# Attention into two dense layers on one core: bias load ahead of keys, another order of units in the last group, the weight split three steps earlier, and another end of attention

## The chip, the cores and the metric

The kernel runs on one core of a Trainium2 chip. The time is device microseconds (us) of one execution; lower is better. A run of the same kernel varies: the three runs of the kernel before lie between 447.11 and 455.0 us. Engines are called as the profile calls them: PE (TensorE matmul), PEld (its weight loads), DVE (VectorE), ACT (ScalarE), POOL (GpSimd) and SP (SyncE, which here issues DMAs; SPq is its queue).

## The reference

Three stages, in float32. Attention over 2 batches, 8 heads, 576 positions and head dimension 64, with a bias that a small network makes from positions; then a dense layer pair with softplus (512 to 2048 to 512); then a layer that sends each token to one of 8 experts or past them.

```python
scores = scale * np.matmul(q, k.transpose(0, 1, 3, 2))
x = (np.log1p(np.abs(rel)) / psi_i)[..., None]
bias = np.maximum(x @ w1 + b1, 0.0) @ w2
scores = scores + bias.transpose(2, 0, 1)[None, :, :, :]
attn = np.exp(scores - np.max(scores, axis=-1, keepdims=True))
attn = attn / (np.sum(attn, axis=-1, keepdims=True) + 1e-09)
attn_out = np.matmul(attn, v)
# ... tokens x 512, then
h = x @ w_in
y = (np.maximum(h, 0.0) + np.log1p(np.exp(-np.abs(h)))) @ w_out
# ... then the routed layer: gate, expert w1 and w2 of each token
```

## The kernel before

Rows of queries are cut into five tiles of 128 (the last, t = 4, has 64). Heads go in pairs (hp, four of them). A **unit** is one tile, one pair of heads and one batch; the half tile t = 4 takes both batches in one unit, called None. There are 36 units. Tiles form four groups, (0), (1), (2) and (3, 4), and the units of a group run pair by pair. For the pair hp = 0 of the last group the order is (3, batch 0), (3, batch 1), (4, both); for the other pairs the half tile comes first: (4, both), (3, batch 0), (3, batch 1).

The order of instructions on every engine is written out by hand up to the end of attention: a loop over steps n = 0 to 39 works on several units at once. In step n:

- DVE adds bias to the scores of unit n and finds their extreme (`maximum`, two instructions, j = 0 and 1); ACT takes the exponentials (`exp`); DVE makes reciprocals and POOL multiplies by them (`divide`). Up to step 16 the divide is in the same step, from LATE = 17 on in the next one.
- PE makes the scores of unit n + 1 (`sc`). The score tiles have two buffers, and one unit takes both.
- PE transposes unit n - 2 into `pt` (one buffer), and ACT copies it into the tile `at` (three buffers; one for each group, pair and batch).
- When all units that make up one (group, pair, batch) are done, three steps after the last of them PE multiplies by the values (`Values.product`, tile `po`, one buffer). In the next step ACT casts `po` to `x0hi` (`high`) and DVE subtracts into `x0lo` (`low`). Only then is `po` free. Of the first pair of the last group both batches are done with the same unit, so both products stand in step 29, the second after `high` and `low` of the first.
- Up to step 21 the bias of later tiles is made as well: DVE `hid`, PE `pb`, ACT `bsb`, and SP stores it in DRAM (`biasd`); SP loads it later for each tile and pair (`bias_load`), up to three units ahead.

Ahead of the loop the bias of tile 0 is made and stored in 8 pieces; then SP loads the second pair of keys (`k_load(1)`, two DMAs), the first values (`v_load(0)`), and the bias of pairs 0 and 1.

**The weight split.** The weights of the dense layers come as float64, and are turned into two float32 parts. `win_split` takes seven instructions for a block f of `w_in`: ACT `cin..m` (absolute value), DVE L130, L131, L132, L134 (`win`), ACT `whi`, DVE `wlo`. The blocks f = 0 to 3 are split during attention by `fill`: block f begins in step FILL + 4 f and ends four steps later; FILL is 23. Their raw loads (`raw_in`, two buffers) are issued by SP at steps FILL - 6 (two) and FILL + 4 f - 4. So block 3 ends in step 39. Blocks from 4 on are split by code behind attention, whose order a scheduler sets, and which may lie between the last instructions of attention.

Then comes the first dense layer: for each of 16 blocks f PE makes 36 matmuls into `ph` (L631, two buffers), ACT and DVE make the softplus (`ea`, `la`, `ua`, `gA`, `gBt`), and the block two further on can begin when `gA` and `gBt` (L648, L650) have read `ph`. Beside it the split goes on, of `w_in` blocks 4 to 15 and of `w_out` (`cout`, `wohi`, `wolo`). Tokens of groups 0 to 2 fill columns 0 to 767, those of the last group the rest; a block's last 12 matmuls read the rest.

Of the kernel before, what the change touches and what calls it, by code (L numbers as in the profile page):

```python
# [31 lines left out]
P = 128  # L32
# [12 lines left out]
LATE = 17  # L45
FILL = 23
DEPTH = 2
# [30 lines left out]
def build(ctx: ExitStack, tc: tile.TileContext, I, out, dbg=None):  # L78
# [84 lines left out]
    with ExitStack() as ac:  # L163
# [81 lines left out]

        def bias_load(t, hp):
            bt = ap3.tile([P, 2, S], F32, tag="bias", name=f"bias{t}_{hp}", bufs=4)
            src = biasd[t][:P * H * BW].rearrange("(q h w) -> q h w", h=H, w=BW)
            nc.sync.dma_start(bt, src[:, 2 * hp:2 * hp + 2, 16:16 + S])
            return bt  # L250
# [24 lines left out]
        class Unit:  # L275
# [33 lines left out]

            def divide(self):  # L310
                nc.vector.tensor_scalar(self.st[:, :, 2], self.st[:, :, 1], 1e-9, None, ALU.add)
                nc.vector.reciprocal(self.st[:, :, 3], self.st[:, :, 2])  # L312
                for j in range(2):
                    nc.gpsimd.tensor_scalar(self.ep[:, j], self.ep[:, j], self.st[:, j, 3:4], 0.0, ALU.mult, ALU.add)  # L314

# [39 lines left out]
        class Values:  # L355
# [4 lines left out]

            def product(self):
                n = group_cols(self.gi)[1]
                at, a5 = self.ats
                po = self.po = ps_o.tile([P, 512], F32, tag="po", name=f"po{self.gi}_{self.hp}_{self.b}")
                for c in range(4):
                    for j in range(2):
                        nc.tensor.matmul(po[64 * j:64 * j + 64, :n], vn[:, self.hp, c, self.b, j, :],  # L367
                                         at[:, j, c, :n], start=(c == 0), stop=False, tile_position=(0, 64 * j))
                for j in range(2):
                    nc.tensor.matmul(po[64 * j:64 * j + 64, :n], v5[:, self.b * 4 + self.hp, j], a5[:, :n],  # L370
                                     start=False, stop=True, tile_position=(0, 64 * j))
# [18 lines left out]
        for gi, ts in enumerate(GROUPS):  # L390
            for hp in range(4):
                for t in ts if hp == 0 else ts[::-1]:
                    for b in (range(B) if qrows(t) == P else (None,)):
                        units.append((gi, t, hp, b))
                        for b_ in range(B) if b is None else (b,):
                            ends[gi, hp, b_] = len(units) - 1
        qs, bts = {}, {}
# [23 lines left out]
        with tc.manual_schedule(engines=order | {nc.sync.engine}):  # L421
# [17 lines left out]
            for k in range(9):  # L439
                x = set_start(k, k % 2) if k < 8 else None  # L440
                if ready:
# [8 lines left out]
                    ready.store()  # L450
                ready = x
            k_load(1)
            v_load(0)
            bts[0, 0] = bias_load(0, 0)
            bts[0, 1] = bias_load(0, 1)
# [25 lines left out]
            for n in range(N + DEPTH + 2):  # L481
# [27 lines left out]

                for x in done[:1]:  # L510
                    x.high()
                if u:
                    u.maximum(0)
                    u.maximum(1)
                if lastV:
                    lastV.turned5()
                if lastU:
                    lastU.divide()
                for x in done[:1]:
                    x.low()  # L520
                fill(n, False)
                if cur:
# [8 lines left out]
                    cur.store()  # L531
                if u:
                    u.exp(0)
# [3 lines left out]
                if nxt:  # L537
                    nxt.room()
                    nxt.hidden(0)
                if u:  # L540
                    u.exp(1)
# [15 lines left out]
                for x in W[:1]:  # L557
                    x.product()
                if V:
# [4 lines left out]
                if u and n < LATE:  # L564
                    u.divide()
                if len(W) > 1:
                    W[0].high()
                    W[0].low()
                    W[1].product()
                    W = W[1:]  # L570
# [677 lines left out]
```

## Time and profile before

| what | value |
|---|---|
| time, median of 3 runs | 450.26 us (447.11, 450.26, 455.0) |
| the profiled execution | 446.41 us, its span 444.7 us |
| busy, share of the span | PE 94%, PEld 73%, DVE 75%, ACT 62%, POOL 16% |
| making of the first bias, start of the loop | to 29 us |
| attention, steps 0 to 39 | 29 to 179.5 us |
| first dense layer (L631) | 179.5 to 284 us |
| second dense layer | 284 to 350 us |
| routing and experts | 350 us to the end |
| granted TensorE clock | 0.997 of full speed (2.4 GHz), mean of the span |

Times in the trace count from the start of the span. Between the span and the profiled execution's time lie 1.7 us. The share of busy time is a mean over stages; what ends the wait of an engine in one stage stands in the brackets of the timeline's rows: idle time before the instruction, and who ended it.

### The profile page before, as it was taken

What the parts mean: (1) busy time and instruction counts of PE and PEld (TensorE: products, weight loads), DVE (VectorE), ACT (ScalarE), POOL (GpSimd) and SP (SyncE); (2) the same over time, 40 slices, a digit from 0 to 9 for tenths busy, and PEclk for the clock granted to TensorE, in tenths of its full rate; (3) what the DMA queues carried; (4) which work ended last, traced back from release to release, by engine and by line L of the source; (5) the groups of instructions that cost most, each with busy time, mean ns of one, the idle gap of its engine ahead of it and who ended that gap; (6) DMA issues with size and microseconds to landing.
All of it is one profiled execution on the core that took longest, in us unless ns stands there. A gap on an engine that the chain in (4) does not pass through costs nothing.

```text
span 444.7 us, 8978 instructions
## 1 busy us (share of the span) xinstructions
PE 419.5 (94%) x3355; PEld 324.7 (73%) x3355; DVE 332.5 (75%) x868; ACT 275.9 (62%) x519; POOL 70.9 (16%) x99
## 2 busy tenths in 40 slices
PE   8979999999999898979999999999999998999994
PEld 5325767676676566979999999977888776887741
DVE  5788788889878685799999999999995334625501
ACT  4787888888899687499988878936442332111010
POOL 3003332334346353000000000000000000201101
PEclk9999999999999999999999999999999999999998
DMA  6799964558875021642321301033340600599700
GB/s 169 206 334 361 312 190 141 165 138 277 232 248 193 27 95 47 200 139 76 109 83 60 96 0 49 1 99 105 129 142 1 247 38 1 217 360 405 279 1 22
DMA packets 38563, 66.60 MB, mean 150 GB/s; under 512 B 4272, under 2 KB 17844, under 8 KB 38512
## 3 DMA queue, kind: packets, MB, share of 16 engines
q1 hardware_dynamic: 37504, 64.38, 44.6%
q10 hardware_dynamic: 592, 0.80, 0.5%
q0 software_dynamic: 416, 0.77, 0.5%
q8 instruction: 28, 0.46, 0.4%
q14 instruction: 23, 0.19, 0.1%
HBM read 49.80 MB, written 16.69 MB: 150 GB/s over the span
## 4 chain that ended last, share of the span: by engine, by line
PE 54%; DVE 9%; ACT 4%; DMA 3%; issue 2%; POOL 0%; POOLq 0%; ACTq 0%; DVEq 0%; SPq 0%
PE ph L631 16%; PE px L664 5%; PE px L665 5%; PE px L666 5%; PE po L367 3%; PE sc L295 2%; PE bhA L971 2%; PE bhB L971 2%; PE byB L979 2%; PE pt L325 1%; DMA xbJ<-out_dram,tiJ 1%; PE sc_None L295 1%; DMA raw_in<-in_moe_w_in_dram 1%; PE prt L731 1%; DVE ua L652 1%
## 5 line engine op out<-in xcount | busy, mean ns | idle before, releaser
L314 POOL TENSOR_SCALAR ep<-ep,st 128x576 f32<-128x576 f32 x64 | 51.3, 813 | 101.3 <-DVE st L312 73.2
L631 PE MATMUL ph<-x0hi,whi 128*128 128x384 f32 x192 | 64.6, 337 | 2.8 <-DVE gBt L650 2.8
L631 PE MATMUL ph<-x0hi,wlo 128*128 128x384 f32 x192 | 64.2, 334 | 0.0
L631 PE MATMUL ph<-x0lo,whi 128*128 128x384 f32 x192 | 64.2, 334 | 0.0
L218 DVE TENSOR_SCALAR hid<-U 128x320 f32<-128x320 f32 (+17 forms) x134 | 55.3, 471 | 2.4 <-PE pb L223 2.3
L295 PE MATMUL sc<-kst,qr 64*128 64x288 f32 x256 | 51.5, 432 | 2.6 <-DVE st L301 1.2
L301 DVE CUSTOM_DVE_ANT_0 ep<-sc,bias 128x576 f32<-128x576 f32 x64 | 45.7, 751 | 5.1 <-POOL ep L314 2.0
L307 ACT ACTIVATE ep<-ep,st 128x576 f32<-128x576 f32 x64 | 49.0, 772 | 0.0
L295 PEld LDWEIGHTS sc<-kst,qr 64*128 64x128 f32 x256 | 28.8, 185 | 26.7 <-issue 12.7
L231 ACT ACTIVATE bsb<-pb,isc 128x287 f32<-128x287 f32 (+31 forms) x72 | 31.7, 493 | 19.3 <-PE pb L223 18.9
L367 PE MATMUL po<-at,vn 128*64 128x128 f32 (+1 forms) x512 | 38.4, 292 | 1.8 <-DVE x0lo L385 1.8
L223 PE MATMUL pb<-hid,pw 128*32 128x512 f32 (+18 forms) x320 | 38.4, 484 | 1.7 <-ACT bsb L231 1.6
L631 PEld LDWEIGHTS ph<-x0hi,whi 128*128 128x128 f32 x192 | 36.0, 188 | 4.3 <-ACT wohi L610 2.7
L631 PEld LDWEIGHTS ph<-x0lo,whi 128*128 128x128 f32 x192 | 36.0, 188 | 0.0
L631 PEld LDWEIGHTS ph<-x0hi,wlo 128*128 128x128 f32 x192 | 36.0, 188 | 0.0
L345 ACT COPY at<-pt 128x512 f32<-128x512 f32 x64 | 34.1, 587 | 1.4 <-PE pt L325 0.7
L367 PEld LDWEIGHTS po<-at,vn 128*64 128x64 f32 x512 | 28.9, 136 | 6.1 <-DVE x0lo L385 2.5
L325 PEld LDWEIGHTS pt<-ident,ep 64*128 64x128 f32 x512 | 26.5, 138 | 6.0 <-POOL ep L314 1.6
L325 PE MATMUL pt<-ident,ep 64*128 64x64 f32 x512 | 29.0, 226 | 1.2 <-ACT at L345 0.9
L672 ACT CAST ghiB<-gBt 128x384 fp32r<-128x384 f32 x16 | 8.2, 513 | 29.0 <-PE px L665 29.0
L664 PE MATMUL px<-wohi,ghiA 128*128 128x512 f32 x64 | 25.0, 391 | 0.0
L665 PE MATMUL px<-wolo,ghiA 128*128 128x512 f32 x64 | 25.0, 390 | 0.0
(415 smaller groups left out, 845.2 us busy)
## 6 DMA issues: line engine op xcount, KB each, us to landing
biasd<-bsb SPq DMA_DIRECT2D x40, 295.5 KB, 3.5
bias<-biasd SPq DMA_DIRECT2D x20, 576.0 KB, 6.1
raw_in<-in_moe_w_in_dram SPq DMA_DIRECT2D x16, 512.0 KB, 4.0
raw_out<-in_moe_w_out_dram SPq DMA_DIRECT2D x16, 512.0 KB, 3.3
ex<-in_moe_w_dram SPq DMA_DIRECT2D x8, 1024.0 KB, 12.3
ew<-in_moe_w_dram SPq DMA_DIRECT2D x4, 1024.0 KB, 6.0
qr<-in_p_q_dram SPq DMA_DIRECT2D x10, 256.0 KB, 4.7
kst<-in_p_k_dram SPq DMA_DIRECT2D x8, 288.0 KB, 5.4
```

Source lines behind the costliest of these rows:

```text
L218: nc.vector.tensor_scalar(self.hid[c][:, :self.R], U[:, :self.R], Lt[:, g:g + 1], 0.0, ALU.add, ALU.max)
L223: nc.tensor.matmul(ps[32 * c:32 * c + 32, :hi - lo], w2b, self.hid[c][:, lo:hi], start=True, stop=True, tile_position=(0, 32 * c))
L295: nc.tensor.matmul(self.sc[j][qs_, c, :288], self.q[js, self.hp, b, qs_], kst[js, self.hp, b, 288 * c:288 * c + 288], start=True, stop=Tru ...
L301: nc.vector.tensor_tensor_reduce(out=self.ep[:, j].rearrange("p (c k) -> p c k", c=2), in0=self.sc[j][:, :, :288], in1=bias.rearrange("p ( ...
L307: nc.scalar.activation(self.ep[:, j], self.ep[:, j], AF.Exp, bias=self.st[:, j, 0:1], scale=-1.0, accum_out=self.st[:, j, 1:2])
L314: nc.gpsimd.tensor_scalar(self.ep[:, j], self.ep[:, j], self.st[:, j, 3:4], 0.0, ALU.mult, ALU.add)
L325: nc.tensor.matmul(self.pt[:, r, c] if c < 8 else p5[r], flat[rs_, o:o + P], ident[rs_, rs_], is_transpose=True, start=True, stop=True, ti ...
L345: nc.scalar.copy(at.rearrange("p j c n -> p (j c) n")[:, :, off:off + 64], self.pt[:, r])
L367: nc.tensor.matmul(po[64 * j:64 * j + 64, :n], vn[:, self.hp, c, self.b, j, :], at[:, j, c, :n], start=(c == 0), stop=False, tile_position ...
L631: nc.tensor.matmul(ph[:, n, :384], ws[:, c, :], xs[xk][:, c, o:o + 384], start=(k == 0), stop=(k == 11))
L664: nc.tensor.matmul(px, ghi[:, cs], wohi[f], start=(f == 0), stop=False)
L665: nc.tensor.matmul(px, ghi[:, cs], wolo[f], start=False, stop=False)
```

## The change

Six edits. The first bias load is issued ahead of `k_load(1)` and `v_load(0)`, as two DMAs of one head each. FILL goes from 23 to 20. In the first pair of the last group the half tile goes between the two batches of tile 3. `high` is written behind `maximum`, and in the last unit's step (35) both exponentials come ahead of `high`. The last unit is divided on DVE, not POOL. The last product is put into the buffer `pb`, not `po`.

```diff
-FILL = 23
+FILL = 20
...
-        def bias_load(t, hp):
+        def bias_load(t, hp, parts=1):
...
-            nc.sync.dma_start(bt, src[:, 2 * hp:2 * hp + 2, 16:16 + S])
+            for j in range(0, 2, 2 // parts):
+                js = slice(j, j + 2 // parts)
+                nc.sync.dma_start(bt[:, js], src[:, 2 * hp:2 * hp + 2, 16:16 + S][:, js])
...
-            def divide(self):
+            def divide(self, eng):
...
-                    nc.gpsimd.tensor_scalar(self.ep[:, j], self.ep[:, j], self.st[:, j, 3:4], 0.0, ALU.mult, ALU.add)
+                    eng.tensor_scalar(self.ep[:, j], self.ep[:, j], self.st[:, j, 3:4], 0.0, ALU.mult, ALU.add)
...
-                for t in ts if hp == 0 else ts[::-1]:
-                    for b in (range(B) if qrows(t) == P else (None,)):
-                        units.append((gi, t, hp, b))
-                        for b_ in range(B) if b is None else (b,):
-                            ends[gi, hp, b_] = len(units) - 1
+                todo = [(gi, t, hp, b) for t in ts[::-1] for b in (range(B) if qrows(t) == P else (None,))]
+                if len(ts) > 1 and hp == 0:
+                    todo[:2] = todo[1::-1]
...
+            bts[0, 0] = bias_load(0, 0, 2)
             k_load(1)
             v_load(0)
-            bts[0, 0] = bias_load(0, 0)
             bts[0, 1] = bias_load(0, 1)
...
-                for x in done[:1]:
-                    x.high()
                 if u:
                     u.maximum(0)
                     u.maximum(1)
+                    if n == N - 1:
+                        u.exp(0)
+                        u.exp(1)
+                for x in done[:1]:
+                    x.high()
                 if lastV:
                     lastV.turned5()
                 if lastU:
-                    lastU.divide()
+                    lastU.divide(nc.vector if n == N else nc.gpsimd)
...
-                    x.product()
+                    x.product(*((ps_b, "pb") if n == N + DEPTH else (ps_o, "po")))
```

On SP, where the bias of tile 0 has been stored (`biasd_61` is tile 0's, `biasd_62` tile 1's; `bias_0` and `bias_1` are the pairs 0 and 1), it stands before as

```order
L244 DMA biasd_61<-bsb_288 16x8x591 x2
L259 DMA kst<-in_p_k_dram 64x2x576 x2
L262 DMA vn<-in_p_v_dram 128x1024
L249 DMA bias_0_308<-biasd_61 128x2x576
L249 DMA bias_1_310<-biasd_61 128x2x576
L244 DMA biasd_62<-bsb_336 16x8x591 x2
```

and with the change as

```order
L244 DMA biasd_61<-bsb_288 16x8x591 x2
L251 DMA bias_0_305<-biasd_61 128x576 x2
L261 DMA kst<-in_p_k_dram 64x2x576 x2
L264 DMA vn<-in_p_v_dram 128x1024
L251 DMA bias_1_311<-biasd_61 128x2x576
L244 DMA biasd_62<-bsb_337 16x8x591 x2
```

The load of pair 0, which waits until all stores of tile 0 have landed, now stands ahead of keys and values.

On PE, in steps 28 and 29 (names are tile, pair and batch, of `po` group, pair and batch; `sc4_2_None` are the scores of the half tile, 8 matmuls, of which the last stands here), before:

```order
L295 MATMUL sc4_2_None_1_2355<-kst_143,qr4_1958 64x288
L325 MATMUL pt4_1_None_2370<-ident_67,ep4_1_None_2201 128x64 x16
L330 MATMUL p5_29_2369<-ident_67,ep4_1_None_2201 128x128
L367 MATMUL po3_0_0_2389<-at3_0_0_2214,vn_144 64x192 x8
L370 MATMUL po3_0_0_2389<-a53_0_0_2215,v5_145 64x192 x2
L367 MATMUL po3_0_1_2403<-at3_0_1_2273,vn_144 64x192 x8
L370 MATMUL po3_0_1_2403<-a53_0_1_2274,v5_145 64x192 x2
L295 MATMUL sc3_2_0_0_2430<-kst_143,qr3_1805 128x288
```

and with the change, the end of step 28 first:

```order
L327 MATMUL pt3_0_1_2330<-ident_67,ep3_0_1_2159 128x64 x16
L332 MATMUL p5_28_2329<-ident_67,ep3_0_1_2159 128x128
L369 MATMUL po3_0_0_2349<-at3_0_0_2226,vn_144 64x192 x8
L372 MATMUL po3_0_0_2349<-a53_0_0_2227,v5_145 64x192 x2
L297 MATMUL sc4_2_None_0_2379<-kst_143,qr4_1891 64x288
...
L327 MATMUL pt4_1_None_2395<-ident_67,ep4_1_None_2213 128x64 x16
L332 MATMUL p5_29_2394<-ident_67,ep4_1_None_2213 128x128
L369 MATMUL po3_0_1_2414<-at3_0_1_2282,vn_144 64x192 x8
L372 MATMUL po3_0_1_2414<-a53_0_1_2283,v5_145 64x192 x2
```

The product of batch 0 moves one step up, to the other side of the scores `sc4_2_None`.

On ACT, at the end of attention (`ep3_3_1` is the last unit's), before:

```order
L381 CAST x0hi1_90<-po3_2_0_2658 128x192
L307 ACTIVATE ep3_3_1_2629,st3_3_1_2630<-ep3_3_1_2629,st3_3_1_2630 128x576 x2
L345 COPY at3_3_0_2683<-pt4_3_None_2688 128x8x64
L345 COPY at3_3_1_2685<-pt4_3_None_2688 128x8x64
L129 ACTIVATE cin3m_2721<-raw_in3_2459 128x512
L381 CAST x0hi1_90<-po3_2_1_2707 128x192
L345 COPY at3_3_0_2683<-pt3_3_0_2734 128x8x64 x2
L129 ACTIVATE cin4m_2879<-raw_in4_2875 128x512
L345 COPY at3_3_1_2685<-pt3_3_1_2757 128x8x64 x2
L381 CAST x0hi1_90<-po3_3_0_2776 128x192
L150 CAST whi3_101<-win3_2719 128x512
L381 CAST x0hi1_90<-po3_3_1_2792 128x192
```

and with the change:

```order
L309 ACTIVATE ep3_3_1_2639,st3_3_1_2640<-ep3_3_1_2639,st3_3_1_2640 128x576 x2
L383 CAST x0hi1_90<-po3_2_0_2668 128x192
L347 COPY at3_3_0_2692<-pt4_3_None_2697 128x8x64
L347 COPY at3_3_1_2694<-pt4_3_None_2697 128x8x64
L150 CAST whi3_101<-win3_2583 128x512
L383 CAST x0hi1_90<-po3_2_1_2716 128x192
L347 COPY at3_3_0_2692<-pt3_3_0_2739 128x8x64 x2
L129 ACTIVATE cin5m_2943<-raw_in5_2939 128x512
L347 COPY at3_3_1_2694<-pt3_3_1_2761 128x8x64 x2
L383 CAST x0hi1_90<-po3_3_0_2780 128x192
L129 ACTIVATE cin6m_3006<-raw_in6_3002 128x512
L383 CAST x0hi1_90<-po3_3_1_2795 128x192
```

The last exponentials stand ahead of the cast of `po3_2_0`, and blocks 5 and 6 of the weights stand where block 4 and nothing stood; `cin4m` is now eleven instructions further up, in step 33. On DVE 14 instructions stand between the last `x0lo` and the first `gA`, where there were 21; the seven that are gone from there stand ahead of it. On SP the raw load of block 6 moves ahead of the first two loads of `w_out`.

## Rows read from the trace of the kernel before

**Rows 1.** Busy time by stretch: us, engine busy (instructions), clock, DMA share, GB/s.

```profile
140.00:152.00 12.00, 10.07 (x121) 6.75 (x117) 8.30 (x28) 8.16 (x20) 5.05 (x6) 1.00 0.44 168
192.00:195.00 3.00, 0.62 (x4) 0.41 (x3) 3.00 (x6) 3.00 (x5) 0.00 (x0) 1.00 0.95 322
195.00:284.00 89.00, 88.58 (x508) 87.57 (x507) 87.52 (x134) 76.77 (x86) 0.00 (x0) 1.00 0.20 60
```

**Rows 2.** Timeline, step 0: start, duration, engine, line, operation; idle before and releaser.

```profile
28.81 0.80 PE L223 MATMUL pb<-hid,pw 128*32 128x352 f32 x8 [1.03 <-ACT bsb L231]
28.96 0.76 DVE L301 CUSTOM_DVE_ANT_0 ep<-sc,bias 128x576 f32<-128x576 f32 x1 [1.57 <-DMA bias<-biasd]
29.75 0.91 ACT L231 ACTIVATE bsb<-pb,isc 128x239 f32<-128x239 f32 x2 [1.00 <-PE pb L223]
```

**Rows 3.** Timeline: loads ahead of the loop on SP, and step 3's scores on PE.

```profile
19.99 1.31 SPq L259 DMA_DIRECT2D kst<-in_p_k_dram  x2
...
22.85 0.91 SPq L249 DMA_DIRECT2D bias<-biasd  x2
...
40.52 1.64 PE L295 MATMUL sc<-kst,qr 64*128 64x288 f32 x7 [0.29 <-PE pb L223]
```

**Rows 4.** Line 259 in the window 31.9 to 33.7 us: the two DMAs of k_load(2).

```profile
L259 SPq DMA_DIRECT2D kst<-in_p_k_dram x2: 639/782/925, 32.0 to 32.7; - x2
...
DMA to landing us min/median/max: 6.5/6.7/6.9
```

**Rows 5.** Timeline, steps 29 to 35: scores, the two products, and what they wait for.

```profile
144.85 1.87 PE L295 MATMUL sc_None<-kst,qr 64*64 64x288 f32 x16 [0.67 <-DVE st L301]
...
150.43 1.52 PE L367 MATMUL po<-at,vn 128*64 128x192 f32 x16 [1.03 <-DVE x0lo L385]
...
152.20 1.24 PE L295 MATMUL sc<-kst,qr 64*128 64x288 f32 x8
...
158.84 1.20 PE L295 MATMUL sc_None<-kst,qr 64*64 64x288 f32 x16
...
169.21 0.71 PE L325 MATMUL pt_None<-ident,ep_None 64*128 64x64 f32 x16
```

**Rows 6.** Timeline: DVE in steps 21 and 22, then the seven instructions of the first split.

```profile
118.68 0.27 DVE L385 TENSOR_TENSOR x0lo<-po,x0hi 128x128 fp32r<-128x128 f32 x1
120.99 0.76 DVE L301 CUSTOM_DVE_ANT_0 ep<-sc,bias 128x576 f32<-128x576 f32 x1 [2.04 <-POOL ep L314]
...
128.74 0.68 ACT L129 ACTIVATE cin0m<-raw_in 128x512 f32<-128x512 f32 x1
...
129.82 0.64 DVE L130 TENSOR_SCALAR cin0m<-cin0m 128x512 f32<-128x512 f32 x1
...
130.50 0.86 DVE L131 TENSOR_SCALAR cin0a<-cin0m 128x512 uint32<-128x512 uint32 x1
...
133.28 0.68 DVE L132 SCALAR_TENSOR_TENSOR cin0a<-raw_in,cin0a 128x512 uint32<-128x512 uint32 x1
...
136.65 0.84 DVE L134 SCALAR_TENSOR_TENSOR win<-raw_in,cin0a 128x512 uint32<-128x512 uint32 x1
...
138.92 0.63 ACT L150 CAST whi<-win 128x512 fp32r<-128x512 f32 x1
...
139.96 0.83 DVE L151 TENSOR_TENSOR wlo<-win,whi 128x512 fp32r<-128x512 f32 x1
```

**Rows 7.** Timeline, PE in steps 37 and 38: last transposes, last product.

```profile
174.14 0.71 PE L325 MATMUL pt<-ident,ep 64*128 64x64 f32 x16 [0.95 <-ACT at L345]
...
177.70 1.52 PE L367 MATMUL po<-at,vn 128*64 128x192 f32 x16 [0.81 <-DVE x0lo L385]
```

**Rows 8.** Timeline, start of the first dense layer.

```profile
178.31 0.37 SPq L142 DMA_DIRECT2D raw_in<-in_moe_w_in_dram  x1
...
182.67 0.66 ACT L129 ACTIVATE cin5m<-raw_in 128x512 f32<-128x512 f32 x1 [2.76 <-DMA raw_in<-in_moe_w_in_dram]
...
194.62 0.41 PE L631 MATMUL ph<-x0hi,whi 128*128 128x384 f32 x1 [2.38 <-DVE gBt L650]
```

More of the change, by code (lines that the diff above doesn't have):

```diff
@@ L359, in __init__, with product @@
                 self.gi, self.hp, self.b, self.ats = gi, hp, b, ats
-            def product(self):
+            def product(self, pool, tag):
                 n = group_cols(self.gi)[1]
                 at, a5 = self.ats
-                po = self.po = ps_o.tile([P, 512], F32, tag="po", name=f"po{self.gi}_{self.hp}_{self.b}")
+                po = self.po = pool.tile([P, 512], F32, tag=tag, name=f"po{self.gi}_{self.hp}_{self.b}")
                 for c in range(4):
@@ L391, in build @@
             for hp in range(4):
-                for t in ts if hp == 0 else ts[::-1]:
-                    for b in (range(B) if qrows(t) == P else (None,)):
-                        units.append((gi, t, hp, b))
-                        for b_ in range(B) if b is None else (b,):
-                            ends[gi, hp, b_] = len(units) - 1
+                todo = [(gi, t, hp, b) for t in ts[::-1] for b in (range(B) if qrows(t) == P else (None,))]
+                if len(ts) > 1 and hp == 0:
+                    todo[:2] = todo[1::-1]
+                for x in todo:
+                    units.append(x)
+                    for b_ in range(B) if x[3] is None else (x[3],):
+                        ends[gi, hp, b_] = len(units) - 1
         qs, bts = {}, {}
@@ L531, in build @@
                     cur.store()
-                if u:
+                if nu:
                     u.exp(0)
@@ L539, in build @@
                     nxt.hidden(0)
-                if u:
+                if nu:
                     u.exp(1)
@@ L564, in build @@
                 if u and n < LATE:
-                    u.divide()
+                    u.divide(nc.gpsimd)
                 if len(W) > 1:
@@ L568, in build @@
                     W[0].low()
-                    W[1].product()
+                    W[1].product(ps_o, "po")
                     W = W[1:]
```

## The prediction

> **What bounds the kernel now.** I read first the windows of busy time [rows 1]. In the first dense layer from 195 us on PE is busy 88.58 of 89 us at the full granted clock, so nothing placed there buys time, and an edit counts only where PE has holes. The same view shows two: 140 to 152 us, with PE busy 10.07 of 12, and 192 to 195 us, with 0.62 of 3 while DVE and ACT have no gap at all. The timeline of each hole, and of step 0, then says in its brackets who ended the wait. There the edits must act; each is priced by that wait and by what is late next. All sums are made against the profiled execution of 446.41 us; it lies 3.85 under the median of 450.26, so I add the difference to the median.
>
> **The first bias load.** In step 0 DVE's first extreme waits 1.57 us for the first bias load [rows 2]. That is what the edit attacks, but the wait is not on the path. Behind the extreme come the exponentials on ACT, and ahead of them ACT must copy the bias product: 29.75 for 0.91 us, after waiting 1.00 for PE's `pb` at 28.81, which itself waited for ACT [rows 2]. So the exponentials start at 30.6 however early the extreme is done at 28.96 + 0.76 + 0.75. I take a gain of 0; its far end is the whole 1.57.
>
> The price is on SP. The load leaves at 22.85, when the last store of tile 0 has landed; `k_load(1)` leaves at 19.99, ahead of that wait [rows 3]. Moved behind it, `k_load(1)`, `v_load(0)` and what SP issues after them start up to 22.85 - 19.99 = 2.86 us later. The first to feel it is `k_load(2)`: issued at 32.0 and 32.7, landing 6.5 to 6.9 later, so by 39.6 [rows 4]; the scores of step 3 start at 40.52 [rows 3]. The slack is 0.9. Some of the 2.86 may come back, because the moved transfers no longer run beside the last stores, which can then land earlier; I take a delay of 1.2, between 0 and 2.86 and nearer to the lower half, hence +0.3 past the slack (0 to 2.86 - 0.9 = 1.96). The edit as a whole: **+0.3**, bounds -1.57 and +1.96.
>
> The Trainium skill speaks against this edit: "DMA: Bandwidth & Descriptors", section "Anatomy of one DMA — SWDGE (gpsimd) path", states that DMA engines do not wait on semaphores and that any such wait happens on the issuing sequencer before dispatch. The issue at 22.85, with nothing from SP after `v_load(0)` until then, agrees [rows 3]. By that rule alone the edit would cost the whole 1.96; if loads could wait in the DMA engines it would cost 0.
>
> **The two products apart.** This is the main term. Three steps with one score of a half tile run from 144.85 to 158.84, 13.99 us, and hold the double product; the next three, which hold the same work but one product less, run from 158.84 to 169.21, 10.37 [rows 5]. The second product waits 1.03 for `x0lo` of the first, since `po` is one buffer, and takes until the next scores at 152.20, 1.77 after its start at 150.43 [rows 5]. With the half tile between the batches, batch 0 is multiplied in step 28 and batch 1 in 29: 3.62 leave the stretch, and 1.77 come back in step 28. There the scores wait 0.67 for DVE [rows 5], and the product now stands ahead of them and covers this wait if the extremes are not late themselves. So the saving is 3.62 - 1.77 = 1.85 to 1.85 + 0.67 = 2.52; the wait is one of DVE, which does not depend on the product, so I take **-2.4**. What is late next there: DVE's extremes, which already end the waits for scores.
>
> **The split three steps earlier.** The first block has seven instructions, 0.68 + 0.64 + 0.86 + 0.68 + 0.84 + 0.63 + 0.83 = 5.16 us [rows 6]; the other blocks meet the same kind of steps as before. The first now starts in step 20. DVE's share there, 0.64 + 0.86, comes behind `x0lo` at 118.68, ahead of the extreme at 120.99 that waits 2.04 for POOL [rows 6]: hidden, and without that wait 1.5. ACT's 0.68 stands ahead of a cast whose result `x0lo` needs, and may push it by a part. I take **+0.2**, bounds 0 and +1.0.
>
> **The end of attention** gains one wait and pays two small ones. The last product waits 0.81 at 177.70 for `x0lo` [rows 7]; in the buffer `pb` it needs not: -0.81. Against it, block 3's pair L130 and L131 now stands in step 33 ahead of the extremes; in rows it costs 0.64 + 0.86 = 1.5 beside POOL, and since `cin3m` may be early I take 0.9 (0 to 1.5). And `cin5m` now stands ahead of the last copies on ACT, while its raw load takes 4.36 from issue at 178.31 to the cast at 182.67 [rows 8]; issued as soon as block 3's `win` is done, it may hold up the copy and with it the last product. I take 0.6 (0 to 2.76, the wait it has now [rows 8]). The division on DVE is hidden behind the 0.95 that the last transposes wait for ACT's copy [rows 7]; were that cover gone, it would cost two instructions of the extreme's size, 0.76 each [rows 2], less POOL's. The exponentials ahead of `high` move `high` later, not the path: 0. Net **+0.7**, bounds -0.81 and +3.4.
>
> **The first dense layer.** PE waits 2.38 us at 194.62 for `gBt` of block 0 [rows 8], because ACT and DVE work off the late splits first: 3.00 of 3 us busy on both [rows 1]. With the split earlier, 14 instead of 21 DVE instructions stand between the last `x0lo` and the first `gA`; seven fewer at 0.43 to 0.86 are 3.0 to 6.0 us, more than the gap. But ACT at 182.67 waits 2.76 for a raw load [rows 8], and the next blocks' loads can bring such a wait back. I take **-2.2**, bounds 0 and -2.38.
>
> **Sum.** 0.3 - 2.4 + 0.2 + 0.7 - 2.2 = -3.4: a profiled execution of 443.0, and 450.26 - 3.4 = **446.9 us** at the median.
>
> **Rivals.** A, the start is on the path after all: if `pb` and the copies of step 0 do move up with the extreme, 1.57 is gained and 0.3 becomes about -1.6: sum -5.3, 445.0 us. Against it stands the order of ACT, where the copy precedes the exponential [rows 2]. Chance 0.12.
>
> B, the hole at 194.62 stays: the loads of block 6 and of the first of `w_out` land late, ACT stands in front of `ea`, and 2.38 is only passed on. The sum is -3.4 + 2.2 = -1.2, 449.1 us. For it speaks the 2.76 wait on a load [rows 8]. Chance 0.16.
>
> C, slower than before: the split moved into steps 20 to 24 is exposed. All 5.16 us on the path in place of 0.2 give -3.4 + 4.96 = +1.6, 451.9 us; it decides from 3.6 us exposed on. It would happen if ACT and DVE, not PE, set those steps. Against it stands the 2.04 in which DVE has nothing to do [rows 6]. Chance 0.10.
>
> D, the split of the products does nothing, as step 28 takes on as much as step 29 loses (its extremes late by the moved product): -3.4 + 2.4 = -1.0, 449.3 us. Against it stands the 1.03 wait, which has no reason to come back when the second product stands a step away. Chance 0.08.
>
> **How the numbers follow.** The forecast has 0.54. The range reaches from the forecast less the outer gains (-3.4 - 1.9 at the start = 445.0, and a further 3.5 for the scatter of the median: three runs lie between 447.11 and 455.0, the lowest 3.15 under the median) to C's 451.9: 441.5 to 452. The bound of 2%, about what a measurement of this kernel can tell from no change, is 441.3 and 459.3. All cases lie within it; faster by more needs A together with the best bounds of the tail (-0.8) and a low draw of the median: 0.11. Slower by more needs C with the bounds of start and tail: 0.03. Within: 0.86.
>
> **What would show it.** Right: the first extreme earlier by about 1.5 us while the first exponential stays at about 30.6; score starts of steps 29 to 32 about 10.4 us apart where they were 13.99, and no wait of PE for `x0lo` between two products; the first matmul into `ph` at about 178 (179.5 less 2.4, plus start, split and tail); no idle time ahead of block 2's first `ph`. Wrong: a wait of step 3's scores on a DMA of over 1 us; scores of steps 21 to 24 further apart; a wait of ACT for `raw_in` ahead of its last copies, or ahead of the first `ea`. The forecast fails on its largest terms, the products and the hole at 194.62, if either wait only moves to another engine.

## The result and the profile after

The changed kernel takes 443.3 us at the median of 20 runs (441.7 to 447.55), the kernel before 449.82 in the same comparison (446.39 to 455.5). The ratio is 0.9876, 95% interval 0.9855 to 0.9898: 1.2% faster, some 5.6 us; the medians lie 6.5 us apart, at the edge of that interval. The profiled execution takes 442.35 us with a span of 440.5; before it was 446.41 and 444.7. The 4.2 us between the spans can be followed by the start of each step's scores on PE, and this is where they arise:

| stretch | forecast, us | profiled, us |
|---|---|---|
| start, to the scores of step 4 | +0.3 | +1.31 (46.09 against 44.78) |
| the split in steps 20 to 24 | +0.2 | +0.04 |
| products, to the scores of step 31 | -2.4 | -2.53 (from +1.31 to -1.22) |
| end of attention, to the first `ph` | +0.7 | -0.39 (177.86 against 179.47, that is -1.61) |
| first dense layer, to block 2 | -2.2 | -2.12 (190.89 against 194.62, that is -3.73) |
| all behind it | 0 | -0.47 |
| sum | -3.4 | -4.2 |

The timeline of the changed kernel up to step 4, of SP, DVE, ACT and PE (start, duration, engine, line; in brackets idle time before and who ended it):

```profile
22.53 0.81 SPq L251 DMA_DIRECT2D bias<-biasd  x2
...
23.39 1.31 SPq L261 DMA_DIRECT2D kst<-in_p_k_dram  x2
...
27.34 0.74 DVE L303 CUSTOM_DVE_ANT_0 ep<-sc,bias 128x576 f32<-128x576 f32 x1
...
30.58 0.77 ACT L309 ACTIVATE ep<-ep,st 128x576 f32<-128x576 f32 x1
...
33.32 1.91 PE L297 MATMUL sc<-kst,qr 64*128 64x288 f32 x8 [1.80 <-DVE st L303]
...
34.72 1.53 SPq L261 DMA_DIRECT2D kst<-in_p_k_dram  x2
...
41.41 0.72 PE L297 MATMUL sc<-kst,qr 64*128 64x288 f32 x2 [0.35 <-DMA kst<-in_p_k_dram]
...
42.51 0.96 PE L297 MATMUL sc<-kst,qr 64*128 64x288 f32 x5 [0.38 <-DVE hid L218]
...
46.09 1.61 PE L297 MATMUL sc<-kst,qr 64*128 64x288 f32 x7
```

The same first exponential, `k_load(2)`, scores of step 1 and scores of step 4 in the kernel before:

```profile
30.55 0.77 ACT L307 ACTIVATE ep<-ep,st 128x576 f32<-128x576 f32 x1
...
31.97 1.62 SPq L259 DMA_DIRECT2D kst<-in_p_k_dram  x2
...
33.28 1.91 PE L295 MATMUL sc<-kst,qr 64*128 64x288 f32 x8 [0.85 <-DMA biasd<-bsb]
...
44.78 1.61 PE L295 MATMUL sc<-kst,qr 64*128 64x288 f32 x7
```

The first extreme comes at 27.34 instead of 28.96 and no longer waits for the bias load, but the first exponential starts at 30.58, where it started at 30.55. `k_load(2)` is issued at 34.72 instead of 31.97, 2.75 us later, and the scores of step 3, which did not wait for it [rows 3], now do: they start 0.89 later than the 40.52 of before, and stop for another 0.38 us at 42.51. The bracket there names a DVE instruction; that this was the second of the two DMAs of keys is read from its issue, 0.7 us behind the first, and not shown by a landing.

Two windows of busy time of the changed kernel (us, busy time of PE, PEld, DVE, ACT and POOL, granted clock, DMA share, GB/s):

```profile
20.00:22.50 2.50, 2.33 (x20) 0.62 (x18) 0.88 (x3) 0.75 (x2) 0.00 (x0) 1.00 0.69 209
...
35.36:38.70 3.34, 3.34 (x17) 1.85 (x13) 2.64 (x9) 1.99 (x5) 1.47 (x2) 0.50 1.05 410
```

The DMA engines have room while SP waits for the last store: their share is 0.69, where the same window of the kernel before has 0.94. From 35.36 to 38.70 the granted clock is 0.50, that is 1.2 GHz, behind the wait of 1.80 us at 33.32. In the kernel before, PE's wait ahead of the same scores was 0.85 us, and the clock stayed at 1.00.

The timeline from step 29 to the first dense layer, PE but for two rows of DVE and one of ACT:

```profile
147.26 1.20 PE L297 MATMUL sc_None<-kst,qr 64*64 64x288 f32 x16
...
151.06 1.24 PE L297 MATMUL sc<-kst,qr 64*128 64x288 f32 x8
...
157.62 1.20 PE L297 MATMUL sc_None<-kst,qr 64*64 64x288 f32 x16
...
162.17 0.73 DVE L130 TENSOR_SCALAR cin3m<-cin3m 128x512 f32<-128x512 f32 x1
162.94 0.43 DVE L131 TENSOR_SCALAR cin3a<-cin3m 128x512 uint32<-128x512 uint32 x1
...
164.09 1.67 PE L297 MATMUL sc<-kst,qr 64*128 64x288 f32 x7 [0.67 <-DVE st L303]
...
169.77 1.52 PE L369 MATMUL po<-at,vn 128*64 128x192 f32 x16 [0.35 <-DVE x0lo L387]
...
173.43 0.71 PE L327 MATMUL pt<-ident,ep 64*128 64x64 f32 x16 [0.91 <-ACT at L347]
...
174.15 0.68 ACT L129 ACTIVATE cin5m<-raw_in 128x512 f32<-128x512 f32 x1 [0.77 <-DMA raw_in<-in_moe_w_in_dram]
...
176.09 1.52 PE L369 MATMUL po<-at,vn 128*64 128x192 f32 x16
...
177.86 0.44 PE L638 MATMUL ph<-x0hi,whi 128*128 128x384 f32 x1
...
190.89 0.41 PE L638 MATMUL ph<-x0hi,whi 128*128 128x384 f32 x1 [0.25 <-DVE gBt L657]
```

From 147.26 to 157.62 are 10.36 us where 13.99 stood [rows 5]: the three steps have become as long as the next three. The last product has no wait (it was 0.81 [rows 7]), and ahead of block 2 stand 0.25 instead of 2.38 us [rows 8]. The first `ph` of the kernel before started at 179.47:

```profile
179.47 0.44 PE L631 MATMUL ph<-x0hi,whi 128*128 128x384 f32 x1
```

### The profile page after: what moved, and what is told of

The parts are those of the page before. It is cut to its first block, busy times and chain, and to the rows that moved or that the text cites. A ratio compares the mean times of both kernels' runs of the same rounds, so it can differ in the third digit from the quotient of the medians.

```text
span 440.5 us, 8980 instructions
## 1 busy us (share of the span) xinstructions
PE 418.5 (95%) x3355; PEld 324.7 (74%) x3355; DVE 333.5 (76%) x870; ACT 275.9 (63%) x519; POOL 70.2 (16%) x97
## 4 chain that ended last, share of the span: by engine, by line
PE 52%; DVE 12%; ACT 4%; DMA 3%; issue 2%; SPq 0%; POOL 0%; POOLq 0%; DVEq 0%; ACTq 0%
PE ph L638 14%; PE px L671 5%; PE px L672 5%; PE px L673 5%; PE po L369 3%; PE sc L297 2%; DMA raw_out<-in_moe_w_out_dram 2%; PE bhA L978 2%; PE bhB L978 2%; PE byB L986 2%; DMA xbJ<-out_dram,tiJ 1%; DVE hid L218 1%; PE sc_None L297 1%; DVE ua L659 1%; PE pt L327 1%
```

## The experiments

Twelve kernels ran. A stretch is read from the profile, since executions differ in slow stretches of the clock (last section) by more than most single edits are worth. Each ratio is to the kernel before, with its 95% interval.

**The first bias load back behind the first values**, the rest as changed:

```diff
-            bts[0, 0] = bias_load(0, 0, 2)
             k_load(1)
             v_load(0)
+            bts[0, 0] = bias_load(0, 0)
```

> The changed kernel with the first bias load put back behind the first values, as before. Theory (the moved load costs 1.30 us between steps 0 and 4): first extreme at about 28.96 again, no granted clock of 0.50 between 35 and 39 us, scores of step 4 at 44.8 instead of 46.09, all later steps 1.3 us earlier; profiled execution about 441.0, ratio to the kernel before about 0.985. Rival (the delay of steps 2 to 4 is due to something else, or is taken back later): scores of step 4 stay at about 46, or the end stays at 442.3, ratio 0.9876.

The timeline and a window of this kernel:

```profile
40.64 1.64 PE L297 MATMUL sc<-kst,qr 64*128 64x288 f32 x7 [0.29 <-PE pb L223]
...
44.90 1.62 PE L297 MATMUL sc<-kst,qr 64*128 64x288 f32 x7
...
373.50:377.00 3.50, 3.50 (x10) 2.68 (x10) 3.33 (x19) 0.51 (x1) 0.00 (x0) 0.51 0.20 18
```

Scores of step 4 at 44.90, no wait for keys, and the last matmul `ph<-x0hi,whi` starts at 278.5 instead of 280.1: the theory holds in all that it can be read from. The profiled execution still takes 442.45, because the clock falls in the routing, at 373.5, and that costs 1.6. Median 442.01, ratio 0.9859 (0.981 to 0.9908): 0.8 us better than 0.9876, with an interval of some 2 us either way, so the two can't be told apart.

**The moved load alone**, in the kernel before (the diff above read the other way round):

> The kernel before with the first bias load moved ahead of keys and values, as in the change, and nothing else. Theory (the moved load pushes k_load(2) past the slack of 0.9 us, and the wait makes the clock fall in some executions): first extreme at 27.3, first exponential still at 30.6; scores of step 4 between 46.0 and 48.5 instead of 44.78, varying from execution to execution; slower than the kernel before by 1.3 to 3.5 us, ratio 1.003 to 1.008. Rival (the start costs only inside the changed kernel, or is taken back in the first steps): scores of step 4 at 44.8, ratio 1.000 or below.

PE's scores in its timeline:

```profile
33.19 1.91 PE L297 MATMUL sc<-kst,qr 64*128 64x288 f32 x8 [1.80 <-DVE st L303]
...
43.30 2.62 PE L297 MATMUL sc<-kst,qr 64*128 64x288 f32 x7 [2.83 <-DMA kst<-in_p_k_dram]
...
48.99 1.41 PE L297 MATMUL sc<-kst,qr 64*128 64x288 f32 x6
```

Slower: 453.46 against 449.77, ratio 1.007 (1.0035 to 1.0105), some 3.1 us. The wait of 2.83 is the one for `k_load(2)`, and the matmuls behind it run at a granted clock of 0.56 to 0.59 from 43 to 47 us. Scores of step 4 come at 48.99, 4.2 us late and half a microsecond later than the theory's end. Five of the profiled kernels have this same code up to step 4 (this one, the changed kernel, and three below); their step 4 stands at 46.09, 46.68, 47.77, 48.99 and 50.11, on average 3.1 us behind 44.78. So the 1.31 of the changed kernel's profile is the cheapest of five draws.

**Exponentials of step 0 ahead of the bias copy on ACT**, in the changed kernel:

```diff
                     u.maximum(1)
-                    if n == N - 1:
+                    if n in (0, N - 1):
                         u.exp(0)
                         u.exp(1)
...
-                if nu:
+                if nu and n:
                     u.exp(0)
...
-                if nu:
+                if nu and n:
                     u.exp(1)
```

> The changed kernel with both exponentials of step 0 ahead of the copy of the bias product on ACT. Theory (the early extreme is worth nothing since ACT takes the copy first, and k_load(2) is the next limit): first exponential at about 28.8 instead of 30.58, scores of step 1 at about 31.8 instead of 33.32 and no slow clock behind them; but the scores of step 3 wait for k_load(2), which lands at 41.3 and about 42.4, so the scores of step 4 come at 45.6 to 46.1 instead of 46.09 and the whole at 441.8 to 442.4, ratio 0.986 to 0.988. Rival (the price of the load was the clock alone): scores of step 4 at 44.5 or earlier, the whole at about 440.8, ratio 0.984.

ACT and PE in the timeline of this kernel:

```profile
28.63 0.77 ACT L309 ACTIVATE ep<-ep,st 128x576 f32<-128x576 f32 x1
...
31.80 1.73 PE L297 MATMUL sc<-kst,qr 64*128 64x288 f32 x8
...
41.54 2.53 PE L297 MATMUL sc<-kst,qr 64*128 64x288 f32 x7 [2.07 <-DVE hid L218]
...
48.46 1.24 PE L297 MATMUL sc<-kst,qr 64*128 64x288 f32 x8
```

The first two parts of the theory show: exponential at 28.63, scores of step 1 at 31.80, 1.5 us earlier. So it was ACT's order that withheld the gain of the early extreme. Step 3 then waits 2.07; the bracket names a DVE instruction that had ended, and `k_load(2)` landed at 41.40, just ahead of the start at 41.54. Step 4 at 48.46 is later than either theory gave: behind the longer wait the clock stays at 0.50 for 6 us. Median 443.71, ratio 0.9882 (0.9825 to 0.9939).

**The same with `k_load(2)` right behind the first two bias loads**, ahead of the values:

```diff
             k_load(1)
+            bts[0, 1] = bias_load(0, 1)
+            k_load(2)
             v_load(0)
-            bts[0, 1] = bias_load(0, 1)
...
-                if n < 2:
-                    k_load(n + 2)
+                if n == 1:
+                    k_load(3)
```

> The changed kernel with both exponentials of step 0 ahead of the copy of the bias product, and the keys of the third pair, k_load(2), issued right behind the first two bias loads instead of in step 0. Theory (the early extreme is worth 1.5 us only if nothing behind it waits for the loads that were pushed back): scores of step 1 at 31.8, of step 3 at about 39.2 without a wait, of step 4 at 43.3 to 43.6 where the changed kernel has 46.09 and the kernel before 44.78; granted clock 1.00 from 30 to 46 us; profiled execution about 439.7, or 441.3 if a slow stretch of the clock falls into the routing. Rival (the load of the values, now behind, is the next limit, or DMA is full until 54 us anyway): scores of step 4 at 45 or later, no better than the kernel before.

PE and DVE in the timeline of this kernel:

```profile
39.83 1.64 PE L297 MATMUL sc<-kst,qr 64*128 64x288 f32 x7 [0.29 <-PE pb L223]
...
44.09 1.61 PE L297 MATMUL sc<-kst,qr 64*128 64x288 f32 x7
...
52.90 0.76 DVE L303 CUSTOM_DVE_ANT_0 ep<-sc,bias 128x576 f32<-128x576 f32 x1 [1.13 <-DMA bias<-biasd]
```

No wait for keys at step 3, and step 4 at 44.09, half a microsecond behind the theory but 0.69 ahead of the kernel before. Then, at 52.90, an extreme waits 1.13 for a later bias load, and from step 6 on the kernel is 0.6 behind the kernel before. The rival's sign, step 4 at 45 or later, did not come; its reason fits what came instead: from 30 to 54 us the DMA engines of the kernel before have a share of 1.06, so that what is moved ahead may make another transfer late. No run shows this apart. The profiled execution, 443.26 with a slow stretch in the routing, is 2 us above the 441.3 expected. Ratio 0.9853 (0.9795 to 0.9912).

**Ten idle matmuls in PE's wait of 1.80 us** (added work that nobody reads):

```diff
+                    if n == 1:
+                        idle = ps_o.tile([P, 512], F32, tag="po", name="idle")
+                        for k in range(10):
+                            nc.tensor.matmul(idle[:, :P], ident, ident, start=True, stop=True)
                     nu.scores()
```

> The changed kernel with ten matmuls of 128 by 128 in step 1 whose result nobody reads, in the 1.80 us in which PE waits ahead of the scores at 33.32. Theory (half of the 1.30 us is the clock that fell behind that wait, half the late k_load(2)): clock 1.00 from 35 to 39 us, scores of step 2 at 36.4 to 36.5, of step 3 at about 41.3, where k_load(2) lands, of step 4 at about 45.5 to 45.7 instead of 46.09. Rival 1 (the clock cost nothing that k_load(2) would not cost anyway): scores of step 4 at 46.0. Rival 2 (all of it is the clock): scores of step 4 at 44.8.

PE at step 3 in the timeline of this kernel:

```profile
45.27 2.67 PE L297 MATMUL sc<-kst,qr 64*128 64x288 f32 x7 [4.93 <-DMA kst<-in_p_k_dram]
```

Inconclusive. The added matmuls take 2.50 us and put the scores of step 1 at 33.95 instead of 33.32. The clock stays at 1.00 from 33 to 43 us, but in this execution `k_load(2)` was issued at 37.01 and landed at 45.1, and the wait of 4.93 swallowed what was to be told apart; step 4 stands at 52.19. Ratio 0.9897 (0.9832 to 0.9962). In the changed kernel's own profile the split of its 1.31 can be read without it: `k_load(2)` landed at 41.28, step 3 began at 41.41, so with a full clock it could have begun 0.13 earlier. There the late keys are the price, and the slow clock ran beneath it.

**The new order of units alone**, in the kernel before:

> The kernel before with the new order of units alone. Theory (one product moved saves 2.5 us and needs none of the other edits): scores of step 30 at 149.7 instead of 152.20, the rest of attention 2.5 us earlier, first dense layer from 177.0; the hole ahead of block 2 stays at 2.4 us or grows a little; profiled execution about 443.9, ratio 0.9945. Rival (the gain needs the split out of these steps): scores of step 30 at 151 or later, ratio 0.997 or more.

PE in the timeline of this kernel, at step 30 and at block 2:

```profile
149.94 1.24 PE L295 MATMUL sc<-kst,qr 64*128 64x288 f32 x8
...
193.22 0.41 PE L633 MATMUL ph<-x0hi,whi 128*128 128x384 f32 x1 [2.48 <-DVE gBt L652]
```

Scores of step 30 at 149.94 where 152.20 stood, while step 24 is 0.20 later: 2.47 us saved, as expected, and by one edit. In the next step 0.31 is lost to an extreme that is late beside the split, so that 2.16 are left, and another 0.45 goes in step 34 in the same way (a wait of 0.65 at 163.33). So the first dense layer starts at 177.96, a microsecond later than expected. The hole of 2.48 remains. Profiled 446.48 with a slow stretch of 1.6 in the routing, where 443.9 was expected; ratio 0.996 (0.9921 to 0.9999).

**FILL = 20 alone**, in the kernel before:

> The kernel before with the split begun three steps earlier and nothing else. Theory (the split's place decides the hole ahead of block 2 of the first dense layer, 2.38 us): hole of 0.3 us or less, steps 20 to 24 not later by more than 0.2 us, profiled execution about 444.3, ratio 0.995. Rival 1 (the last unit's edits closed the hole): hole above 1.5 us, ratio 0.999. Rival 2 (the split is exposed in the last steps of attention): hole closed, but the first dense layer starts at 180.2 or later, ratio 0.997 or more.

PE in the timeline of this kernel, at step 34 and at the first dense layer:

```profile
164.62 1.67 PE L295 MATMUL sc<-kst,qr 64*128 64x288 f32 x7 [0.67 <-DVE st L301]
...
179.39 0.45 PE L631 MATMUL ph<-x0hi,whi 128*128 128x384 f32 x1
```

No row of the first dense layer in this timeline has a wait in brackets: the hole is gone, by this edit alone. Steps 20 to 24 are not later (0.10 us behind the kernel before, and 0.05 before them), steps 29 to 33 are 0.7 earlier, because the wait of 0.67 ahead of the scores at 144.85 [rows 5] is gone; it is the one that the moved product covers, so the two edits do not add up there. Of the 0.7, 0.47 goes at 164.62, where the extremes stand behind the pair L130 and L131. Ratio 0.9911 (0.9871 to 0.9951), the largest of the parts.

**FILL = 23 in the changed kernel**:

> The changed kernel with the split begun in step 23 again. Theory (the split's place alone closes the hole ahead of block 2, and costs two tenths in steps 20 to 24): attention no later, first dense layer from 177.4 to 177.9, but a wait of 2.2 to 2.8 us ahead of block 2 in place of 0.25; total about 2.2 us longer, ratio 0.992. Rival (the order of the last steps closes it as well): wait below 1.2 us, ratio 0.989 or less.

PE at step 34, at a product of step 35 and at block 2 in the timeline of this kernel:

```profile
164.81 1.67 PE L297 MATMUL sc<-kst,qr 64*128 64x288 f32 x7 [0.65 <-DVE st L303]
...
171.01 1.52 PE L369 MATMUL po<-at,vn 128*64 128x192 f32 x16 [0.86 <-DVE x0lo L387]
...
193.98 0.41 PE L638 MATMUL ph<-x0hi,whi 128*128 128x384 f32 x1 [2.25 <-DVE gBt L657]
```

The hole is back with 2.25 us; ratio 0.9951 (0.9908 to 0.9994), 3.4 us slower than the changed kernel's, where 0.992 was expected. The first dense layer starts at 178.97, outside the expected 177.4 to 177.9 and 1.11 behind the changed kernel: 0.59 of it comes from the start (step 4 stands at 46.68), and 0.51 from the product at 171.01, which waits 0.86 for `x0lo` where the changed kernel waits 0.35. The wait of 0.65 at step 34 is there as well, with the split in its old place. Behind the hole the granted clock falls to 0.50, from 195 to 197 us.

**The last product in `po` again**:

```diff
-                    x.product(*((ps_b, "pb") if n == N + DEPTH else (ps_o, "po")))
+                    x.product(ps_o, "po")
```

> The changed kernel with the last product in the buffer po again. Theory (the other buffer saves the wait of 0.81 us): a wait of 0.8 us for x0lo ahead of the last product, first dense layer from 178.6 to 178.7 instead of 177.86, the rest of attention unchanged, total 0.8 us longer if the hole ahead of block 2 does not take it up (it has 0.25 left). Rival (ACT's copy behind block 5 is late anyway): start of the dense layer unchanged within 0.2 us.

The last product in the timeline of this kernel:

```profile
178.89 1.52 PE L369 MATMUL po<-at,vn 128*64 128x192 f32 x16 [0.81 <-DVE x0lo L387]
```

The 0.81 is back to the digit. From the scores of step 34 to the first `ph` it takes 165.99 to 180.67, 14.68 us, against 13.77 in the changed kernel (and 14.63 before). The start at 180.67 instead of 178.6 is mostly due to a late step 4 (47.77 instead of 46.09). Ratio 0.9925 (0.9888 to 0.9962).

**The last unit divided on POOL**:

```diff
-                    lastU.divide(nc.vector if n == N else nc.gpsimd)
+                    lastU.divide(nc.gpsimd)
```

> The changed kernel with the last unit divided on POOL. Theory (the division is hidden by the wait of the last transposes for ACT's copy): start of the last transposes and of the first dense layer, counted from the scores of step 34, as in the changed kernel (13.77 us to the dense layer) within 0.2 us. Rival (POOL's 1.5 to 1.7 us for the pair is late): dense layer 0.5 us later or more, counted in the same way.

The last transposes in the timeline of this kernel:

```profile
178.46 0.71 PE L327 MATMUL pt<-ident,ep 64*128 64x64 f32 x16 [0.96 <-ACT at L347]
```

The last transposes wait 0.96 for the same copy as with DVE (0.91), and from step 34 to the dense layer it takes 13.92 (169.07 to 182.99): 0.15 more, within the 0.2. The division on DVE buys nearly nothing. On POOL the pair takes 2.33 us and ends at 178.56, after the transposes have begun; the two on DVE take 0.94 and end 0.86 ahead of them. Ratio 0.9897 (0.9858 to 0.9935), with step 4 at 50.11, the latest of the five.

**Keys and values of the second and first pair issued at 7 us**, behind the first queries:

```diff
             qs[0] = q_load(0)
+            k_load(1)
+            v_load(0)
...
             bts[0, 0] = bias_load(0, 0, 2)
-            k_load(1)
-            v_load(0)
             bts[0, 1] = bias_load(0, 1)
```

> The changed kernel with k_load(1) and v_load(0) issued behind the first queries, at about 7 us, where the DMA engines have room, so that nothing of them stands behind the wait of the moved load. Theory (what costs is the time that the DMA engines lose between 20 and 22.8 us): k_load(2) issued at 32 us or earlier, no wait for it at step 3, scores of step 4 at 44.7 to 45.0, clock 1.00 there; profiled execution about 441.0, or 442.6 with a slow stretch in the routing; ratio 0.982 to 0.986. Rival (the extra transfers delay the stores of the first bias, and with them the moved load): first extreme at 28.5 or later and scores of step 4 at 45.5 or later.

The scores of steps 3 and 4 in the timeline of this kernel:

```profile
40.50 1.71 PE L297 MATMUL sc<-kst,qr 64*128 64x288 f32 x7 [0.37 <-DMA kst<-in_p_k_dram]
...
44.82 1.61 PE L297 MATMUL sc<-kst,qr 64*128 64x288 f32 x7
```

Step 4 at 44.82: the price of the moved load is gone, though step 3 still waits 0.37. `k_load(2)` was issued at 33.72 and not by 32. The clock stays at 1.00, although the same wait of 1.80 us stands at 33.18. A good microsecond is lost later: at 132.30 an extreme waits 1.77 us for a bias load, with a DMA share of 1.00 to 1.05 from 130 to 136 us, and from step 4 to the first `ph` this kernel takes 132.76 us where the changed kernel takes 131.77 and the next one 131.65. Median 442.95, ratio 0.9831 (0.9784 to 0.9878).

**The same with the exponentials of step 0 first**:

> As the kernel with keys and values early, and both exponentials of step 0 ahead of the copy of the bias product. Theory (with the transfers out of the way the early extreme is worth what ACT's order withheld): scores of step 1 at 31.8, of step 3 at about 39.5 without a wait for k_load(2), of step 4 at 43.4 to 43.8; profiled execution about 439.7 (441.3 with a slow stretch in the routing), ratio 0.979 to 0.983. Rival (DMA is full until 54 us, so that an earlier start only waits at a later step): scores of step 8 no earlier than with keys early alone, ratio equal to it within 0.002.

The same two in the timeline of this kernel:

```profile
40.20 1.75 PE L297 MATMUL sc<-kst,qr 64*128 64x288 f32 x7 [0.63 <-DMA kst<-in_p_k_dram]
...
44.57 1.61 PE L297 MATMUL sc<-kst,qr 64*128 64x288 f32 x7
```

Step 1 at 31.89, but step 3 waits for `k_load(2)`, which lands at 40.06, and step 4 comes at 44.57, 0.25 ahead of the kernel above instead of 1.3. In step 8 it is still 0.25 ahead (61.45 against 61.70), and the ratios are within 0.002. So the rival holds but for this quarter: the early start mostly waits later. The profiled execution is the shortest seen, 439.91, with no slow stretch in the routing and no wait like the one at 132.30; median 442.1, ratio 0.984 (0.9797 to 0.9883). Neither of the two can be told from the changed kernel by its interval.

## Why the prediction came out as it did

It gave 446.9 us, range 441.5 to 452, most chance to a change within 2%; the median is 443.3. The direction and the two main steps held, and the sum was too small. That the profiled sum, -4.2, lies so near to -3.4 is in part luck: the start came out 1.0 us worse than forecast and the end of attention 1.1 us better.

**Products and dense layer** were read rightly. For -2.4 the changed kernel shows -2.53, and the order of units alone -2.47. The mechanism shows too: the scores at 147.26 have no wait and are 2.41 behind the 144.85 of before [rows 5], 1.31 of it from the start; the 1.10 left (1.08 with the units alone) is the moved product of 1.77 less the wait of 0.67 that it covers. The hole was priced at -2.2 and measured at -2.12; the kernel with FILL = 20 alone shows that the split's place closes it, and the one with FILL = 23 that the other edits do not. Rivals B and D fall with these. The split in steps 20 to 24 cost 0.04 where 0.2 was given, so C falls too.

**The start was the step that was mis-sized on the bad side.** That 1.57 is no gain, since ACT copies first, was right (rival A falls), and putting the exponentials first showed it. But the delay of 1.2 us taken for `k_load(2)` was an arbitrary point between 0 and 2.86; issue was 2.75 us later in the changed kernel, close to the upper end, so the slack of 0.9 was passed by more. The upper bound of 1.96 failed as well: three of the five profiled executions with this code, and the load moved alone with 3.1 us at the median, lie above it. The bound took the delay of SP from one trace: with the load moved alone, the load left at 23.79 and `k_load(2)` at 37.26, 5.3 us later than before. And it left out that the clock can be low behind a wait of PE, which adds to the wait: behind 2.83 us it was 0.50 from 44 to 46 us with the load moved alone. In the changed kernel the 3.1 us are neither confirmed nor refuted, since putting the load back gives 0.8 with an interval of 2 either way. With keys and values issued at 7 us no price is left at step 4. The prediction weighed a rule of the Trainium skill, "DMA: Bandwidth & Descriptors", "Anatomy of one DMA — SWDGE (gpsimd) path", that a semaphore wait happens on the issuing sequencer. The trace of SP's queue agrees: `k_load(1)`, which left at 19.99 [rows 3], left at 23.39, right behind the waiting load at 22.53.

**The end of attention was mis-sized on the good side**: +0.7 forecast, -0.39 measured. The buffer gave the 0.81 forecast. For the pair L130 and L131 I took 0.9; the scores of step 34 wait 0.67 where 0.20 stood, 0.47 more. But it is not the pair's new place alone that costs this: with FILL = 23 in the changed kernel, and with the units alone, the same wait is 0.65, behind L132, which there takes 1.16 and 1.17 us instead of 0.68. Either edit brings the wait by itself (0.67 with FILL = 20 alone), and both together leave 0.67; why L132 is longer there stays open. For `cin5m` I took 0.6: it does wait 0.77 for its raw load, one of the prediction's signs of being wrong, but the copy behind it is done by 175.8, while PE is busy until 176.09 with the product before. This is a cover that the trace of before has (a product at 175.04) and that I did not count. Of the exponentials ahead of `high` I took 0: the product at 169.77 now waits 0.35 for `x0lo`, yet from the scores of step 34 to the last transposes it takes 9.34 us against 9.30 before, so the sum holds. No run takes this edit back alone.

**What stays open** is part of the size. Terms summed in the profile give -4.2; the comparison of 20 runs each gives 1.24%, 5.6 us. The profiled execution of the kernel before, 446.41, is next to the lowest of its runs (446.39), while that of the changed kernel, 442.35, lies nearer its median; so the profiles understate the distance between medians. One candidate stands in the profiles: of the four with the hole ahead of block 2, two (the moved load alone, FILL = 23 in the changed kernel) have the granted clock at 0.50 behind it, and take 90.5 and 90.0 us from block 2 to the last `ph<-x0hi,whi`, where the kernel before takes 89.0. If the low clock is the hole's doing, the hole cost 1.0 to 1.5 more in these executions than in the profile of before. How much of the 1.4 us this makes can't be said, as the longer executions of before have no profile.

## What to carry to other kernels

A transfer that waits for a store should not be issued ahead of transfers that wait for nothing: the whole queue stands behind it. That the bandwidth lost meanwhile is missing later, where DMA is full, fits the runs but is argued. Before a wait is attacked, look at what the engine that takes the result still has in front of it; here ACT's order made 1.57 us worth nothing. And when one group of work is split over two buffers or two steps, read the price from two stretches of the same work with and without it, as the 13.99 and 10.37 us here.

## What the hardware showed

The granted clock fell to 0.50 (1.2 GHz) in the middle of work, after a wait of PE, but not after each. In the changed kernel it was 0.50 from 35.36 to 38.70 behind a wait of 1.80 us, and with FILL = 23 it fell behind the same wait; with keys early, and in the three other profiles with it, the same wait was followed by 1.00. Behind the waits ahead of step 3, of 1.69, 1.71, 2.07, 2.83 and 4.93 us in five profiles, it fell each time. Behind the hole ahead of block 2 it fell after 2.25 and 3.06 us and not after 2.38 and 2.48. In the routing, behind two short waits of PE (0.87 and 0.30 us, with the same length in all), 8 of the 14 profiled executions of this study show such a stretch: matmuls of 512 columns start 0.43 us apart instead of 0.23, and from the matmul into `pcntA` to the one into `tgpA`, two tiles of the routing, it takes 8.1 us instead of 6.5. Kernels with one edit have it as well as kernels with all but one; the profiles of the kernel before and of the changed kernel do not. So it is 1.6 us of scatter between single profiles.
